# A spectral layer and gated FFN on one core: from unit 8 on, frequency units go in pairs, with a fourth buffer for loaded units

## The chip, the cores and the metric

The kernel runs on one core of a Trainium2 chip. The metric is the device time of one execution in microseconds (us); the core has a matrix engine (PE, with its weight loads shown apart as PEld), a vector engine (DVE), an activation engine (ACT), GpSimd (POOL), and SyncE (SP), which here issues all DMAs. The time before is the median of three runs.

## The reference

```
X = np.fft.rfft(x, axis=1)                      # x: 8 x 3136 x 256
Yr = Xr @ w_r - Xi @ w_i + b_r
Yi = Xr @ w_i + Xi @ w_r + b_i
Yr, Yi = soft-threshold of both at lam = 0.01
y = np.fft.irfft(Yr + 1j * Yi, n=3136, axis=1)
h = np.maximum(y @ w_in, 0.0)                   # 256 -> 1024
conv_out = 3-tap depthwise convolution of h along the sequence
out = (h * sigmoid(conv_out)) @ w_out           # 1024 -> 256
```

The weights of the second half (`w_in`, `conv_w`, `w_out`) arrive as 64-bit floats, which the kernel takes apart as bit patterns on VectorE into a high and a low part.

## The kernel before

The transform of length 3136 is done as 49 by 64. **Stage 1** transforms along 49: for each of 64 *pieces* (8 of them to a batch row) the PE runs `quads` (L333) on a loaded tile `xr`, ACT and DVE copy the two result banks to `a1` (L350, L351), and every second piece is stored to DRAM with three DMAs (L338, L342). **Stage 2** works on *units* of four frequencies: there are 50 (six to a batch row, and one more for each four rows that holds the last frequency). A unit loads its `a2` tile (L371), transforms along 64 on the PE in two halves (L384), and splits the result: ACT copies and casts (`d` L387, `fh` L388), DVE subtracts (`d` L389, `fl` L390), then `third` adds a third plane, on ACT (L395) and POOL (L396). The **mix** multiplies a unit by the complex weights as three planes of 12 matmuls (L412) into three PSUM banks, and DVE joins them to `v` with two additions of the bias (L415) and two of the planes (L417). `shrink` is the soft threshold: two passes of ACT (L428, L429) and one of POOL (L430); the last unit uses `clip` on DVE (L422, L423). **Stage 3** transforms back along 64 (L440, L443) into the pool `psa`, which has one buffer of two banks; ACT copies it to `z1` (L450, two buffers), and DMAs store it (L455, L458). All other PSUM of this part is a ring of six banks, handed out in program order.

`later()` is a generator of *weight steps*: eight pieces of `w_in` and `w_out` of ten DVE steps each, and three short ones for `conv_w`. In the ninth step of a piece DVE subtracts (L279) what ACT has cast in the same step (L278).

The order is written out by hand: engines execute in program order. One turn of the main loop holds stage 3 of unit `it-4`, one or two pieces of stage 1, stage 2 of unit `it`, `shrink` of unit `it-2` and the mix of unit `it-1`. So the mix multiplies what stage 2 made one turn earlier, and three weight steps of DVE stand around the copies of stage 1. Pieces run in turns 1 to 40. From unit 45 on, `last_stage` (stage 4, the way back along 49 for batch row 0, L159; ACT L168, DVE L170) fills the places that pieces had. Then the **FFN** starts: `up` (L656) makes 128 rows of h for two column halves in PSUM (`ps_h`), ACT and DVE make the gate, and `down` (L691) sums into `acc`. Its pools take over the eight PSUM banks: the first `ps_h` lies in banks that were the ring's.

SP issues DMAs in the order of the program too, and waits in front of each for its buffer or its data: whatever is asked later stands behind it.

## Time and profile before

| | us |
|---|---|
| median of 3 runs (1671.15 to 1673.64) | 1672.62 |
| the profiled execution | 1672.12 |
| its span, first to last instruction | 1670.3 |
| PE busy | 1655.1 |
| DVE busy | 1388.5 |
| ACT busy | 1176.6 |
| POOL busy | 192.3 |
| FFN's first matmul (L656) | 468.76 after the span's start |

The profile is of one execution. An engine's busy time is the union of its instructions' records. A row of the timeline gives the start and the length in us of instructions that follow each other, merged when they are alike; the length of a matmul's record reaches past the start of the next, so the pace is read from starts. A row of windows gives, for a stretch, each engine's busy time, the granted clock of the PE (1.00 is full) and the DMA engines' busy share. In the program's names of the profile, digits are left out: `ps_s` is the PSUM tile of stages 1 to 4, `z` of stage 3's store, `a` of stage 1's and of stage 2's load.

### The profile page before, as it was taken

How to read it: one execution, taken by the hardware profiler on the slowest of the kernel's cores; microseconds unless marked ns; L12 is line 12 of the kernel's file. 1: busy time of each engine (PE TensorE's matmuls, PEld its weight loads, DVE VectorE, ACT ScalarE, POOL GpSimd, SP SyncE). 2: the span in 40 equal slices, each digit the busy share in tenths (PEclk: the TensorE clock that was granted, in tenths of full speed). 3: DMA queues.
4: the chain of work that ended last, by engine and by line, in shares of the span. 5: the costliest groups of instructions: out<-in, count | busy, mean ns of one | idle time of the engine just before them, and what ended most of it. 6: DMA issues, size and time to landing. Idle time of an engine off the chain costs nothing.

```text
span 1670.3 us, 30664 instructions
## 1 busy us (share of the span) xinstructions
PE 1655.1 (99%) x12618; PEld 1539.5 (92%) x12618; DVE 1388.5 (83%) x1728; ACT 1176.6 (70%) x1585; POOL 192.3 (12%) x114
## 2 busy tenths in 40 slices
PE   9899999999999999999999999999999999999998
PEld 6688888889999999999999999999999999999998
DVE  3578988877688888888888888888888888888887
ACT  3577777777677777677777776777777776777776
POOL 1444444445300000000000000000000000000000
PEclk9999999999999999999999999999999999999999
DMA  8999999887421101111111011111001111100001
GB/s 219 285 293 283 261 262 275 257 224 195 118 71 52 52 33 42 52 52 42 49 34 44 32 31 52 42 52 52 33 33 52 46 38 52 42 23 23 23 23 45
DMA packets 108297, 162.29 MB, mean 97 GB/s; under 512 B 10842, under 2 KB 87806, under 8 KB 108094
## 3 DMA queue, kind: packets, MB, share of 16 engines
q1 hardware_dynamic: 108158, 160.34, 32.6%
q8 instruction: 100, 1.64, 0.4%
q14 instruction: 39, 0.32, 0.1%
HBM read 83.24 MB, written 77.07 MB: 96 GB/s over the span
## 4 chain that ended last, share of the span: by engine, by line
PE 98%; DMA 1%; issue 0%; ACT 0%; SPq 0%; ACTq 0%
PE acc L691 33%; PE ps_h L656 33%; PE ps_mx L412 13%; PE ps_s L159 7%; PE ps_s L384 6%; PE ps_s L333 3%; PE ps_s L440 3%; PE ps_idle L509 0%; DMA hx<-in_x_dram 0%; DMA a<-sch 0%; PE ps_s L443 0%; DMA sch<-ha 0%; SPq L316 0%; ACT o L697 0%; SPq L319 0%
## 5 line engine op out<-in xcount | busy, mean ns | idle before, releaser
L691 PE MATMUL acc<-wout,gh 128*128 128x256 f32 x3136 | 565.4, 281 | 0.4 <-ACT gh L677 0.4
L672 DVE SCALAR_TENSOR_TENSOR c<-h,cw,c 128x896 f32<-128x896 f32 x448 | 512.8, 1147 | 63.0 <-ACT c L670 61.8
L656 PE MATMUL ps_h<-yh,win 128*128 128x450 f32 (+1 forms) x1792 | 545.0, 365 | 0.0
L691 PEld LDWEIGHTS acc<-wout,gh 128*128 128x128 f32 x3136 | 490.1, 188 | 5.9 <-ACT gh L677 0.6
L691 PE MATMUL acc<-wout,gl 128*128 128x256 f32 x1568 | 434.7, 279 | 0.0
L666 ACT ACTIVATE h<-ps_h 128x898 f32<-128x898 f32 (+1 forms) x224 | 207.2, 925 | 226.7 <-PE ps_h L656 226.4
L656 PEld LDWEIGHTS ps_h<-yh,win 128*128 128x128 f32 x1792 | 337.1, 188 | 24.0 <-issue 0.4
L656 PE MATMUL ps_h<-yl,win 128*128 128x450 f32 (+1 forms) x896 | 327.8, 366 | 0.0
L691 PEld LDWEIGHTS acc<-wout,gl 128*128 128x128 f32 x1568 | 293.3, 188 | 0.2
L674 DVE TENSOR_TENSOR c<-h,c 128x896 f32<-128x896 f32 x224 | 243.4, 1087 | 47.7 <-ACT c L673 46.7
L678 DVE TENSOR_TENSOR gl<-c,gh 128x896 fp32r<-128x896 f32 x224 | 243.2, 1088 | 33.5 <-ACT gh L677 30.1
L677 ACT CAST gh<-c 128x896 fp32r<-128x896 f32 x224 | 210.4, 944 | 81.3 <-DVE c L674 81.1
L673 ACT ACTIVATE c<-c 128x896 f32<-128x896 f32 x224 | 213.5, 954 | 24.1 <-DVE c L672 21.3
L656 PEld LDWEIGHTS ps_h<-yl,win 128*128 128x128 f32 x896 | 168.4, 188 | 10.2
L670 ACT ACTIVATE c<-h,cw 128x896 f32<-128x896 f32 x168 | 175.4, 1044 | 2.9 <-DVE gl L678 0.2
L412 PE MATMUL ps_mx<-wmix_hi,fh 128*128 128x256 f32 x600 | 172.1, 287 | 0.0
L412 PE MATMUL ps_mx<-wmix_lo,fh 128*128 128x256 f32 x600 | 167.6, 279 | 0.0
L412 PE MATMUL ps_mx<-wmix_hi,fl 128*128 128x256 f32 x600 | 167.2, 279 | 0.0
L430 POOL TENSOR_TENSOR r<-r,v 128x1024 f32<-128x1024 f32 x48 | 114.6, 2387 | 217.7 <-ACT v L429 200.1
L384 PEld LDWEIGHTS ps_s<-t,a 128*128 128x128 f32 (+1 forms) x800 | 94.4, 194 | 37.7 <-issue 22.8
L159 PEld LDWEIGHTS ps_s<-i,z 98*128 98x128 f32 x1024 | 122.5, 192 | 2.0 <-issue 0.8
L159 PE MATMUL ps_s<-i,z 98*128 98x98 f32 x1024 | 123.3, 273 | 0.0
(93 smaller groups left out, 1675.7 us busy)
## 6 DMA issues: line engine op xcount, KB each, us to landing
z<-sc SPq DMA_DIRECT2D x64, 392.0 KB
sc<-z SPq DMA_DIRECT2D x96, 256.0 KB
out_dram<-o SPq DMA_DIRECT2D x27, 896.0 KB
xr<-in_x_dram SPq DMA_DIRECT2D x112, 192.0 KB
sc<-a SPq DMA_DIRECT2D x56, 384.0 KB
a<-sc SPq DMA_DIRECT2D x42, 512.0 KB
hx<-in_x_dram SPq DMA_DIRECT2D x16, 192.0 KB
a<-sch SPq DMA_DIRECT2D x6, 512.0 KB
```

The lines of the kernel that those rows point to most:

```text
L159: nc.tensor.matmul(to, z2[:, j, t * P:(t + 1) * P], i2[:, 0 if jg or j else 1, :], start=(j == 0), stop=(j == JG - 1), skip_group_check=True)
L384: nc.tensor.matmul(ps[:, k], a2[0:kk, k, t * P:(t + 1) * P], t2[0:kk, q, :], start=(k == 0), stop=(k == UG - 1), skip_group_check=True)
L412: nc.tensor.matmul(ps[c][:, k, :], lt, rh, start=(n == 0), stop=(n == len(mm) - 1))
L656: nc.tensor.matmul(dst, lt, rh, start=(i == 0), stop=(i == len(mm) - 1))
L666: nc.scalar.activation(hv, src, AF.Relu)
L670: nc.scalar.mul(cv, tap(0), cw[:, 0, f:f + 1])
L672: nc.vector.scalar_tensor_tensor(cv, tap(k), cw[:, k, f:f + 1], cv, op0=ALU.mult, op1=ALU.add)
L673: nc.scalar.activation(c, c, AF.Sigmoid)
L674: nc.vector.tensor_tensor(cv, tap(1), cv, op=ALU.mult)
L677: nc.scalar.copy(gh, c)
L678: nc.vector.tensor_tensor(gl, c, gh.bitcast(F32), op=ALU.subtract)
L691: nc.tensor.matmul(acc[m // 2][:, m % 2, :], lt[:, sl], rh[:, f, :], start=(f == 0 and n == 0 and m % 2 == 0), stop=(f == NF - 1 and n == ...
```

## The change

The loop is cut in three: turns 0 to 7 as before; from unit 8 on one turn takes two units `u` and `u+1`; a drain of its own at the end. In a turn of two, the PE runs stage 3 of `u-4`, up to two pieces, stage 3 of `u-3`, the rest of the pieces, stage 2 of both units, and the mix of **the same** two units. Each unit's `shrink` follows the mix one unit later. The planes of a paired mix are made in the order 0, 1, 2 rather than 2, 0, 1, and the bias is added to planes 0 and 1. Six weight steps a turn stand as three ahead of stage 3's copy, two ahead of the first mix's additions and one between the two mixes. Where there are no pieces, the second stage 3 of a turn takes two banks of the ring in place of `psa`, and so does stage 3 of the last unit. `a2` has four buffers. Loads of `a2` for the next turn are asked ahead of x, and x is asked for once ahead of the pieces and once behind them.

The rows that follow are the order of instructions, engine by engine, as built. **PE**, around unit 12 (`ps_s_1667` is stage 3 of unit 8, `ps_s_1676` to `1683` pieces of stage 1, `ps_s_1706` and `1715` the halves of unit 12's stage 2); before:

```order
L412 MATMUL ps_mx_1623<-wmix_hi,fl 128x256
L440 MATMUL ps_s_1667<-r,i_465 64x256 x8
L333 MATMUL ps_s_1676<-xr,f_118 64x512 x2
L333 MATMUL ps_s_1677<-xr,f_118 64x512 x2
L333 MATMUL ps_s_1682<-xr,f_118 64x512 x2
L333 MATMUL ps_s_1683<-xr,f_118 64x512 x2
L384 MATMUL ps_s_1706<-t_122,a_1559 128x128 x4
L384 MATMUL ps_s_1715<-t_122,a_1559 128x128 x4
L412 MATMUL ps_mx_1730<-wmix_hi,fh 128x256
```

The same place with the change (`ps_s_1717`, stage 3 of unit 8, stands just ahead; `ps_s_1753` is stage 3 of unit 9, `ps_s_1792` to `1824` stage 2 of units 12 and 13, `ps_mx_1841` the first plane of unit 12's mix):

```order
L333 MATMUL ps_s_1726<-xr,f_118 64x512 x2
L333 MATMUL ps_s_1727<-xr,f_118 64x512 x2
L333 MATMUL ps_s_1732<-xr,f_118 64x512 x2
L333 MATMUL ps_s_1733<-xr,f_118 64x512 x2
L457 MATMUL ps_s_1753<-r,i_465 64x256 x8
L333 MATMUL ps_s_1762<-xr,f_118 64x512 x2
L333 MATMUL ps_s_1763<-xr,f_118 64x512 x2
L384 MATMUL ps_s_1792<-t_122,a_1552 128x128 x4
L384 MATMUL ps_s_1801<-t_122,a_1552 128x128 x4
L384 MATMUL ps_s_1815<-t_122,a_1554 128x128 x4
L384 MATMUL ps_s_1824<-t_122,a_1554 128x128 x4
L413 MATMUL ps_mx_1841<-wmix_hi,fh 128x256
```

The matmuls of 64 rows now stand together, and a mix follows the stage 2 that feeds it.

**ACT and DVE**, where the third weight piece comes to its ninth step. ACT before, around unit 17 (`z_2231` is stage 3's copy, L278 the cast of the weights, `ps_s_2245` and `2254` the halves of stage 2):

```order
L450 COPY z_2231<-ps_s_2216 128x1024
L350 COPY a_2236<-ps_s_2225 128x2x256
L278 CAST win_82<-win_m 128x512
L387 COPY d<-ps_s_2245 128x256
L388 CAST fh<-ps_s_2245 128x512
L387 COPY d<-ps_s_2254 128x256
L388 CAST fh<-ps_s_2254 128x512
L428 ACTIVATE r<-v,small 128x1024
```

ACT with the change, at the end of the turn of units 16 and 17 (the first L441 and L442 are `shrink` of unit 15, the second of unit 16, `z_2397` and `z_2424` stage 3's copies of the next turn):

```order
L388 CAST fh<-ps_s_2250 128x512
L395 CAST fh<-d 128x2x256
L441 ACTIVATE r<-v,small 128x1024
L442 ACTIVATE v<-v,small 128x1024
L278 CAST win_82<-win_m 128x512
L441 ACTIVATE r<-v,small 128x1024
L442 ACTIVATE v<-v,small 128x1024
L471 COPY z_2397<-ps_s_2365 128x1024
L350 COPY a_2189<-ps_s_2374 128x2x256
L350 COPY a_2406<-ps_s_2380 128x2x256
L471 COPY z_2424<-ps_s_2409 128x1024
```

DVE at that place with the change (`ps_s_2250` is stage 2 of unit 17, `ps_mx_2268` to `2270` the planes of unit 16):

```order
L390 TENSOR_TENSOR fl<-ps_s_2250,fh 128x512
L271 SCALAR_TENSOR_TENSOR win_rest<-win_r,win_e 128x512
L279 TENSOR_TENSOR win_m<-win_m,win_82 128x512
L417 TENSOR_TENSOR v<-ps_mx_2268,bias 128x512
L417 TENSOR_TENSOR v<-ps_mx_2269,bias 128x512
L420 TENSOR_TENSOR v<-ps_mx_2270,v 128x512 x2
```

The cast L278 moved from behind stage 3's copy to behind a `shrink`, and L279, which needs it, now stands ahead of the additions of a mix.

**ACT where the FFN starts**, with the change (`ps_s_5834` is the last half of stage 4, `ps_s_5843` stage 3 of unit 48 in `psa`, `ps_s_5852` and `5853` the two ring banks of stage 3 of unit 49; in brackets the semaphores waited for):

```order
L168 CAST yh<-ps_s_5834 128x49x4 [waits PE_49]
L168 CAST yh<-ps_s_5834 128x49x4
L471 COPY z_5862<-ps_s_5843 128x1024 [waits DMAHW4_49,DMAHW5_49,PE_49,Activation_49]
L469 COPY z_5866<-ps_s_5852 64x512 [waits DMAHW0_49,DMAHW1_49,PE_49,Activation_49]
L469 COPY z_5866<-ps_s_5853 64x512 [waits PE_49]
```

DMAHW0 and DMAHW1 are the two stores of unit 47's `z`, whose buffer `z_5866` takes. Stage 3 of unit 49 lay in `psa` before, and the FFN's first `ps_h` waited for stage 4's `yh` and `yl` alone; now unit 49 lies in ring banks that `ps_h` takes over, and the first `ps_h` matmul (L727) waits for the last of these copies.

The diff:

```diff
--- before.py
+++ after.py
@@ -178,7 +178,7 @@
         s1p = eb.enter_context(tc.tile_pool(name="s1p", bufs=2, side="right"))
         c0 = eb.enter_context(tc.tile_pool(name="c0", bufs=1, side="right"))
         c1 = ab.enter_context(tc.tile_pool(name="c1", bufs=1))
-        a2p = ab.enter_context(tc.tile_pool(name="a2p", bufs=3))
+        a2p = ab.enter_context(tc.tile_pool(name="a2p", bufs=4))
         cmx = ab.enter_context(tc.tile_pool(name="cmx", bufs=1))
         DB, XRB = 2, 3
         psx = ab.enter_context(tc.tile_pool(name="psx", bufs=6, space=PSUM))
@@ -396,12 +396,13 @@
             nc.gpsimd.tensor_tensor(fl[:, :, 2], d, fh[:, :, 2].bitcast(F32), op=ALU.subtract)
             return fh, fl
 
-        def mix(xs):
+        def mix(xs, paired=False):
 
 
             fh, fl = xs
-            ps = {c: psx.tile([K2, UG // 2, D], F32, name=f"ps_mx{c}", tag="bank") for c in (2, 0, 1)}
-            for c in (2, 0, 1):
+            order = (0, 1, 2) if paired else (2, 0, 1)
+            ps = {c: psx.tile([K2, UG // 2, D], F32, name=f"ps_mx{c}", tag="bank") for c in order}
+            for c in order:
...
             v = wk.tile([K2, 2, UG // 2, D], F32, name="v")
-            for c in range(2):
-                nc.vector.tensor_tensor(v[:, c], ps[2], bias[:, c:c + 1, :].to_broadcast([K2, UG // 2, D]), op=ALU.add)
-            for c in range(2):
-                nc.vector.tensor_tensor(v[:, c], ps[c], v[:, c], op=ALU.add)
+
+            def biased(c, src):
+                nc.vector.tensor_tensor(v[:, c], ps[src], bias[:, c:c + 1, :].to_broadcast([K2, UG // 2, D]), op=ALU.add)
+
+            def joined(c, src):
+                nc.vector.tensor_tensor(v[:, c], ps[src], v[:, c], op=ALU.add)
+            if paired:
+                for c in range(2):
+                    biased(c, c)
+                for c in range(2):
+                    joined(c, 2)
+            else:
+                for c in range(2):
+                    biased(c, 2)
+                for c in range(2):
+                    joined(c, c)
             return v
 
         def clip(v):
@@ -430,24 +443,32 @@
             nc.gpsimd.tensor_tensor(r, r, v, op=ALU.subtract)
             return r
 
-        def stage3_pe(g, r):
-            ps = psa.tile([P, 2, UG // 2, D], F32, name="ps_s3")
+        def stage3_pe(g, r, ring=False):
+            if ring:
+                ps = [psx.tile([P, UG // 2, D], F32, name="ps_s3", tag="bank") for _ in range(2)]
+            else:
+                both = psa.tile([P, 2, UG // 2, D], F32, name="ps_s3")
+                ps = [both[:, h] for h in range(2)]
             for a in range(2):
                 for k in range(UG // 2):
                     for h in range(2):
                         rows = slice(SP * h, SP * (h + 1))
                         if g < NG:
-                            nc.tensor.matmul(ps[SP * a:SP * (a + 1), h, k, :], i1[rows, a, g * UG // 2 + k, :], r[rows, a, k, :],
+                            nc.tensor.matmul(ps[h][SP * a:SP * (a + 1), k, :], i1[rows, a, g * UG // 2 + k, :], r[rows, a, k, :],
                                              start=(k == 0), stop=(k == UG // 2 - 1), skip_group_check=True)
                         else:
-                            nc.tensor.matmul(ps[0:SP, h, k, :], i1[rows, a, U // 2, :], r[rows, a, k, :],
+                            nc.tensor.matmul(ps[h][0:SP, k, :], i1[rows, a, U // 2, :], r[rows, a, k, :],
                                              start=(a + k == 0), stop=(a + k == UG // 2), skip_group_check=True)
-            return ps
+            return ps if ring else both
 
         def stage3_out(b, g, ps):
             z1 = io.tile([P, 2, UG // 2, D], F32, name="z1", bufs=2)
             n = P if g < NG else SP
-            nc.scalar.copy(z1[0:n], ps[0:n])
+            if isinstance(ps, list):
+                for h in range(2):
+                    nc.scalar.copy(z1[0:n, h], ps[h][0:n])
+            else:
+                nc.scalar.copy(z1[0:n], ps[0:n])
             if g < NG:
                 z1 = z1.rearrange("p h k e -> p (h k) e")
                 for c in range(2):
@@ -469,7 +490,7 @@
 
         items = [(b, g) for h in range(B // BH) for b, g in [(h * BH + b, g) for b in range(BH) for g in range(NG)] + [(h * BH, NG)]]
         n_it, n_pc = len(items), B * NX
-        LAG, WP0, LATE, NW, NF0, NF1 = 4, 8, 10, 7, 14, 3
+        LAG, PAIR, WP0, LATE, NW, NF0, NF1 = 4, 8, 8, 10, 7, 14, 3
         xs, vs, ss, a2s, xq, pair = {}, {}, {}, {}, {}, []
         p1 = nx = NX
 
@@ -551,7 +572,7 @@
         wkf.tile([P, 56], F32, name="pad", bufs=1)
         wk.tile([P, 72], F32, name="pad", bufs=1)
         background = later()
-        Y0, Y1 = n_it - 6, n_it - 1
+        Y0 = n_it - 6
         jgs = iter(range(NPC))
 
         def one_by_one():
@@ -568,65 +589,115 @@
             stage4(jg, z2, y0, one_by_one)
             ask_z2()
 
-        for it in range(n_it + LAG):
-            drain = it >= n_it
+        def steps(n):
+            for _ in range(n):
+                next(background, None)
+
+        def s3(i, ring=False):
+            b, g = items[i]
+            return b, g, stage3_pe(g, ss.pop(i), ring)
+
+        def pieces(n):
+            nonlocal p1
+            todo = [next_s1(p1 + i) for i in range(n)]
+            yield
+            for ps in todo:
+                stage1_out(p1, ps)
+                p1 += 1
+
+        for it in range(PAIR):
...
             if it >= LAG:
-                g3 = items[it - LAG]
-                ps3 = stage3_pe(g3[1], ss.pop(it - LAG))
-            n_s1 = min(2 if 0 < it < 5 else (1, 2, 1, 1, 2, 1)[(it - 5) % 6] if it else 0, n_pc - p1)
-            ps1 = [next_s1(p1 + i) for i in range(n_s1)] if it > 1 else []
+                z = s3(it - LAG)
+            n_s1 = 2 if 0 < it < 5 else (1, 2, 1, 1, 2, 1)[(it - 5) % 6] if it else 0
+            if it > 1:
+                out1 = pieces(n_s1)
+                next(out1)
             if it >= LAG:
-                stage3_out(*g3, ps3)
-            if WP0 <= it < Y0:
-                next(background, None)
-            elif it == WP0 - 2:
-                next(background)
-            for ps in ps1:
-                stage1_out(p1, ps)
-                p1 += 1
+                stage3_out(*z)
+            if it == WP0 - 2:
+                steps(1)
+            if it > 1:
+                next(out1, None)
             ask_a2(it + 1)
-            if WP0 <= it < Y0:
-                for _ in range(2):
-                    next(background, None)
-            if it < n_it:
-                xs[it] = stage2(items[it][1], a2s.pop(it))
-            if it == Y0:
+            xs[it] = stage2(items[it][1], a2s.pop(it))
+            if it >= 2:
+                ss[it - 2] = shrink(vs.pop(it - 2))
+            xs[it] = third(xs[it])
+            if it == 1:
+                out1 = pieces(n_s1)
+                next(out1)
+                next(out1, None)
+            if 0 <= it - 3 < NG:
+                fill_inv1(it - 3)
+            if it:
+                vs[it - 1] = mix(xs.pop(it - 1))
+
+        for u in range(PAIR, n_it, 2):
+            busy = u < Y0
+            ask_a2(u + 2, u + 3)
+            fetch(2)
+            if u == LATE:
+                load_t2(NG)
+                load_inv1(NG)
+            n_s1 = min(sum((1, 2, 1, 1, 2, 1)[(i - 5) % 6] for i in (u, u + 1)), n_pc - p1)
+            if u - 3 < NG:
+                fill_inv1(u - 3)
+            z = s3(u - LAG)
+            out1 = pieces(min(n_s1, 2))
+            next(out1)
+            if busy:
+                steps(3)
+            stage3_out(*z)
+            next(out1, None)
+            z = s3(u + 1 - LAG, not n_s1)
+            out1 = pieces(max(n_s1 - 2, 0))
+            next(out1)
+            stage3_out(*z)
+            next(out1, None)
+            ask_a2(u + 2, u + 3)
+            fetch(2)
+            if u == PAIR:
+                ss[u - 2] = shrink(vs.pop(u - 2))
+                vs[u - 1] = mix(xs.pop(u - 1))
+            for i in (u, u + 1):
+                xs[i] = third(stage2(items[i][1], a2s.pop(i)))
+                if u > Y0:
+                    last_stage()
+            if u == Y0:
                 eb.close()
                 zio, y_a = pool("zio", 3, side="right"), pool("y_a", side="right")
                 y0 = new_y(y_a)
                 z2s = []
                 for _ in range(3):
                     ask_z2()
-            if it == n_it - 1:
-                xs[it] = third(xs[it])
-            if 0 <= it - 2 < n_it:
-                ss[it - 2] = (clip if drain else shrink)(vs.pop(it - 2))
-            if it < n_it - 1:
-                xs[it] = third(xs[it])
-            if Y0 < it < Y1:
-                last_stage()
-            if it == 1:
-                for _ in range(n_s1):
-                    stage1_out(p1, next_s1(p1))
-                    p1 += 1
-            if 0 <= it - 3 < NG:
-                fill_inv1(it - 3)
-            if 0 <= it - 1 < n_it:
-                vs[it - 1] = mix(xs.pop(it - 1))
+            ss[u - 1] = shrink(vs.pop(u - 1))
+            if busy:
+                steps(2)
+            vs[u] = mix(xs.pop(u), True)
+            ss[u] = shrink(vs.pop(u))
+            if busy:
+                steps(1)
+            vs[u + 1] = mix(xs.pop(u + 1), True)
+
+        for n in range(2):
+            z = s3(n_it - LAG + n)
+            last_stage()
+            stage3_out(*z)
+            if n == 0:
+                ss[n_it - 1] = clip(vs.pop(n_it - 1))
+            last_stage()
+        z = [s3(n_it - 2 + n, n) for n in range(2)]
+        for q in z:
+            stage3_out(*q)
         assert p1 == n_pc and not z2s and next(background, True)
 
     wk, hp, io, y_b = pool("cwk"), pool("chp", 3), pool("cio"), pool("y_b")
```

More of the change, by code (lines that the diff above doesn't have):

```diff
@@ L576, in spectral_ffn_kernel @@
                 load_t2(it + 2)
-            elif it == LATE:
-                load_t2(NG)
-                load_inv1(NG)
             if 0 <= it - 2 < NG and it % 2 == 0:
@@ L584, in spectral_ffn_kernel @@
                 fill_t2(it + 1)
-            if drain:
-                last_stage()
             if it >= LAG:
-                g3 = items[it - LAG]
-                ps3 = stage3_pe(g3[1], ss.pop(it - LAG))
-            n_s1 = min(2 if 0 < it < 5 else (1, 2, 1, 1, 2, 1)[(it - 5) % 6] if it else 0, n_pc - p1)
-            ps1 = [next_s1(p1 + i) for i in range(n_s1)] if it > 1 else []
-            if it >= LAG:
-                stage3_out(*g3, ps3)
-            if WP0 <= it < Y0:
-                next(background, None)
-            elif it == WP0 - 2:
-                next(background)
@@ L613, in spectral_ffn_kernel @@
                     ask_z2()
-            if it == n_it - 1:
-                xs[it] = third(xs[it])
-            if 0 <= it - 2 < n_it:
-                ss[it - 2] = (clip if drain else shrink)(vs.pop(it - 2))
-            if it < n_it - 1:
-                xs[it] = third(xs[it])
-            if Y0 < it < Y1:
-                last_stage()
-            if it == 1:
-                for _ in range(n_s1):
-                    stage1_out(p1, next_s1(p1))
-                    p1 += 1
-            if 0 <= it - 3 < NG:
-                fill_inv1(it - 3)
-            if 0 <= it - 1 < n_it:
-                vs[it - 1] = mix(xs.pop(it - 1))
+            ss[u - 1] = shrink(vs.pop(u - 1))
[16 more added lines that the diff above has]
+            stage3_out(*q)
         assert p1 == n_pc and not z2s and next(background, True)
```

## The prediction

> **What bounds the kernel now.** I read the page first: the busy shares by slice, the granted clock, the chain of work that ended last.
>
> ```profile
> PE   9899999999999999999999999999999999999998
> PEclk9999999999999999999999999999999999999999
> PE 98%; DMA 1%; issue 0%; ACT 0%; SPq 0%; ACTq 0%
> L333 PE MATMUL ps_s<-xr,f 49*64 49x512 f32 x448 | 58.4, 594 | 6.9 <-issue 6.3 <-PE ps_s L384 0.5
> 304.08:329.19 25.11, 25.11 (x238) 21.16 (x237) 21.09 (x37) 18.78 (x29) 11.45 (x7) 1.00 0.88 254
> ```
>
> The PE is busy from end to end and its clock nearly always full, and 98% of the chain is PE. The row of groups says that stage 1 (L333) never waited for an `xr` in flight; the waits view shows nothing for the PE from unit 8 to the FFN. The last row is three units of the middle in the view of windows: PE 25.11 of 25.11 us, DVE 21.09, ACT 18.78, DMA engines 0.88 busy. So no wait can be removed. The change can gain only where matmuls that follow each other cost more than their own pace, and it can lose wherever DVE, ACT or a DMA, each with some 15 to 25% to spare, now comes later than the PE wants it.
>
> **What the change removes: changeovers of the PE.** The timeline, starts and lengths:
>
> ```profile
> 303.75 0.28 PE L412 MATMUL ps_mx<-wmix_lo,fh 128*128 128x256 f32 x1
> 303.87 0.28 PE L412 MATMUL ps_mx<-wmix_hi,fl 128*128 128x256 f32 x1
> 304.08 1.11 PE L440 MATMUL ps_s<-r,i 64*64 64x256 f32 x16
> 305.00 1.05 PE L333 MATMUL ps_s<-xr,f 49*64 49x512 f32 x8
> 305.98 2.05 PE L384 MATMUL ps_s<-t,a 128*128 128x128 f32 x16
> 307.79 0.36 PE L412 MATMUL ps_mx<-wmix_hi,fh 128*128 128x256 f32 x1
> 307.99 0.28 PE L412 MATMUL ps_mx<-wmix_lo,fh 128*128 128x256 f32 x1
> ...
> 386.73 1.11 PE L440 MATMUL ps_s<-r,i 64*64 64x256 f32 x16
> 387.77 2.05 PE L384 MATMUL ps_s<-t,a 128*128 128x128 f32 x16
> ...
> 305.98 0.38 PE L384 MATMUL ps_s<-t,a 128*128 128x128 f32 x1
> ...
> L384 PE MATMUL ps_s<-t,a 128*128 128x128 f32 x768 | 99.6, 284 | 0.9 <-DMA a<-sch 0.9
> ```
>
> A unit has one change from tiles of 128 rows (the mix) to tiles of 64 (stage 3, stage 1), and one back (to stage 2). From the start of a mix's last matmul to stage 3 are 304.08 − 303.87 = 0.21 us, where matmuls of the mix follow each other after 303.87 − 303.75 = 0.12: 0.09 lost. Sixteen matmuls of stage 3 take 387.77 − 386.73 = 1.04 ahead of stage 2 and 305.00 − 304.08 = 0.92 ahead of stage 1: 0.12 lost. The first matmul of stage 2 lasts 0.38 against a mean of 0.284: 0.10 more. Sure is 0.09 + 0.12 = 0.21, all three are 0.31, and some 0.05 may lie in the slower first matmuls of stage 3, which this view doesn't part: 0.36 at most. I take 0.34, near the three. A turn of two units saves one such pair: stage 2 to stage 2, mix to mix, and stage 3 among the pieces stay in one size of tile. That is 21 turns, and one more in the drain, where stage 3 of units 48 and 49 stand together: 22 × 0.34 = **7.5 us** (22 × 0.21 = 4.6 to 22 × 0.36 = 7.9). Nothing else of the PE's work is changed in number.
>
> **What it adds: waits.** The mix now multiplies what stage 2 has just made. Stage 2 as it went before, from its start S = 305.98:
>
> ```profile
> 307.23 0.37 ACT L387 COPY d<-ps_s 128x256 f32<-128x256 f32 x1 [0.45 <-PE ps_s L384]
> ...
> 308.34 0.59 ACT L388 CAST fh<-ps_s 128x512 fp32r<-128x512 f32 x1
> ...
> 308.18 0.42 DVE L389 TENSOR_TENSOR d<-ps_s,d 128x256 f32<-128x256 f32 x1 [0.37 <-issue]
> ...
> 309.45 0.68 DVE L390 TENSOR_TENSOR fl<-ps_s,fh 128x512 fp32r<-128x512 f32 x1
> ```
>
> ACT's splits run from S + 1.25 to S + 2.95, and DVE's, one behind the other, from S + 2.2 to 309.45 + 0.68 = S + 4.15. Unit u's mix starts two stages 2 later, at S + 2 × (307.79 − 305.98) = S + 3.62. Its first matmul takes 0.20 and the next ones 0.12 each, so the sixth, the first to take the second half's `fl`, is due at S + 4.3, and its weight load, which carries `fl`, 0.12 earlier. So `fl` and the need for it meet within 0.05 us. DVE's steps ahead of it (stage 1's copies, three weight steps) are over by then on an even turn, or up to 0.2 late. I take 0.08 a turn: 21 × 0.08 = **1.7** (0 to 21 × 0.25 = 5). Behind ACT's splits of u come those of u+1, behind DVE's too; their mix is due 2.9 us later and is covered.
>
> Stage 3 of the turn's second unit uses the one buffer of `psa`, and so waits for ACT's copy of the first one's. That copy stands behind two `shrink`s.
>
> ```profile
> 305.28 1.01 ACT L450 COPY z<-ps_s 128x1024 f32<-128x1024 f32 x1 [1.73 <-PE ps_s L440]
> ...
> 308.81 1.16 ACT L428 ACTIVATE r<-v,small 128x1024 f32<-128x1024 f32 x1
> 310.01 1.15 ACT L429 ACTIVATE v<-v,small 128x1024 f32<-128x1024 f32 x1
> ...
> L417 DVE TENSOR_TENSOR v<-ps_mx,v 128x512 f32<-128x512 f32 x100 | 67.7, 684 | 14.8 <-PE ps_mx L412 14.8
> ...
> L278 ACT CAST win<-win_m 128x512 fp32r<-128x512 f32 x4 | 2.5, 630 | 0.0
> L279 DVE TENSOR_TENSOR win_m<-win_m,win 128x512 f32<-128x512 f32 x4 | 2.7, 685 | 2.5 <-ACT win L278 2.5
> ```
>
> From the first mix's start M: a mix is 312.17 − 307.79 = 4.4 us; its last plane is whole at about M + 4.5, DVE's two joins (2 × 0.68, L417) end at M + 5.9, the two passes of `shrink` (1.16 + 1.15) at M + 8.3. Stage 3 of u−4 starts after both mixes, at M + 8.5 or so, ends at M + 9.5, and its copy (1.01) at M + 10.7. With two pieces between (each 305.98 − 305.00 = 0.95) stage 3 of u−3 is due at M + 8.5 + 0.9 + 1.8 = M + 11.2, after it. Where the ninth step of a weight piece is one of the two ahead of the mix's additions, the order shown above has L278 behind a whole `shrink` on ACT and L279 ahead of L417 on DVE: the additions start some 3 us late, `shrink` ends some 2 us late, and the copy at M + 12.4, so that stage 3 waits 1.2 or so. This is so for the third and the sixth of the eight pieces (one with fewer pieces of stage 1 behind it, half of that). In the turn with one piece left it is due at M + 10.3 and waits 0.5. Sum **2.4** (0.5 if DVE gets ahead in time, 4 if each lasts twice as long).
>
> The start of the FFN:
>
> ```profile
> 463.90 1.11 PE L440 MATMUL ps_s<-r,i 64*64 64x256 f32 x16
> 464.93 2.03 PE L159 MATMUL ps_s<-i,z 98*128 98x98 f32 x16
> 466.89 1.94 PE L443 MATMUL ps_s<-r,i 64*64 64x256 f32 x16
> 468.76 0.47 PE L656 MATMUL ps_h<-yh,win 128*128 128x448 f32 x1
> ...
> 446.76 1.08 SPq L455 DMA_DIRECT2D sc<-z  x2
> ...
> 449.50:450.50 1.00, 1.00 (x11) 1.00 (x10) 1.00 (x3) 1.00 (x2) 0.59 (x1) 1.00 0.41 156
> 450.50:451.50 1.00, 1.00 (x10) 1.00 (x10) 1.00 (x2) 0.97 (x2) 0.71 (x1) 1.00 0.00 0
> ```
>
> Let T be the start of unit 47's stage 3. Then come two stages 4 (466.89 − 464.93 = 1.96 each), stage 3 of 48 and 49 (0.92 + 1.87), and the PE is free for `ps_h` at T + 1.04 + 3.9 + 2.8 = T + 7.7. On ACT unit 47's copy stands behind four casts of the stage 4 before and the first of the next, and ends at about T + 4.6. Its buffer's next user, the copy of unit 49, waits for both stores. A pair of stores (446.76) left the DMA engines idle some 3.7 us after it was asked: 0.41 busy in the slice from 449.50, 0.00 in the next. So unit 49's two half copies start at T + 8.4 and end 2 × 0.59 later (a copy of 512 elements from PSUM is as long as L388 above), at T + 9.6; `ps_h` waits for them, as it lies in their banks. **2.0 us** of a wait that was not there (1 to 3: what the stores take).
>
> The fourth `a2` buffer and the earlier requests take nothing off the PE, which did not wait for `a`; moved weight steps are the same DVE work. What they could cost is rival C.
>
> Sum: −7.5 + 1.7 + 2.4 + 2.0 = −1.4. Against the profiled execution, 1672.12, that is 1670.7; the median lies 0.50 above it, so **1671.2 us**.
>
> **Rivals.** *A, no waits but the last.* DVE is idle 16% of a unit and makes `fl` in time; the weight steps fall well; the gain stands against the FFN's 2.0 and some 1: 1672.6 − 7.5 + 3.0 = 1668.1. For it: `fl` is due within 0.05 us of its making, and the bounds at zero. Against: two of the waits follow from program order alone. Chance 0.26.
>
> *B, the clock.* The PE's idle time at the FFN's start could cost more than itself:
>
> ```profile
> 7.40:10.80 3.40, 1.93 (x12) 0.42 (x8) 0.93 (x2) 0.58 (x1) 0.00 (x0) 1.00 1.01 200
> 10.90:17.60 6.70, 6.70 (x70) 5.11 (x70) 1.38 (x2) 1.17 (x2) 0.00 (x0) 0.50 1.00 243
> ...
> 41.60:45.00 3.40, 2.38 (x16) 0.93 (x15) 0.00 (x0) 0.75 (x2) 1.14 (x2) 1.00 1.03 324
> ```
>
> Here 3.40 us with the PE 1.93 busy were followed by 6.7 at a granted clock of 0.50; 3.40 us with 2.38 busy still ran at full clock. [...] Half the clock for 6.8 us is up to 3.4 us more: 1674.6. Chance 0.22. [...]
>
> *C, x comes late, slower.*
>
> ```profile
> 303.85 2.77 SPq L316 DMA_DIRECT2D xr<-in_x_dram  x4
> 306.67 0.56 SPq L319 DMA_DIRECT2D xr<-in_x_dram  x1
> ```
>
> Such a load holds two pieces, in one of three buffers. Eight pieces pass in six units, 2 × 25.11 us, so two pieces in 12.6. When a load is asked, at least one buffer is still full: 12.6 less 3.4 to ask it and some 3.7 to land (as the stores above) leaves a lead of at least 5.5 us. The change asks `a2` of the next two units ahead of x, and where a batch row begins, those wait for the last stores of stage 1, with x behind them on SP: if each of the two waits a whole landing, 2 × 3.7 = 7.4 us, x is up to 1.9 late; I price it at half, 1 us, at the five row starts that follow unit 8: 1671.2 + 5 = 1676.2. It decides from a delay of 5.5 us. For it: the DMA share of 0.88. Against: stage 1 never waited for x under way, and x is asked twice a turn. Chance 0.10. That the change doesn't do what it says is excluded by the rows of the order.
>
> **How the numbers follow.** Forecast 0.42, A 0.26, B 0.22, C 0.10. About 0.2%, 3.3 us, is what a measurement can tell from no change. Faster by more than that means below 1669.3: all of A and a little of the forecast's range (0.01), 0.27. Slower means above 1675.9: C (0.10) and the half of B where other terms come out high (0.10), 0.20. The rest is 0.53. The forecast's own range, by the bounds of its terms, is 1668 to 1674.5; A's lower end (gain 7.9, costs 2) is 1667, C's middle with a little more 1677. So 1667 to 1677.
>
> **What would show it.** Two mixes side by side in the timeline, and stage 3 to stage 2 with one changeover a turn. Waits of the PE's weight loads for DVE's `fl`, some 0.1 each; of stage 3 for ACT's `z`, one or two near 1 us; of the first `ps_h` for ACT's `z`, about 2. A wait of L279 for L278 in the first half, twice 2 us. The FFN's first matmul at about 467.4 in place of 468.76. Granted clock 0.50 right behind it would be B; any wait of L333 for DMA `xr` would be C. Wrong would be the prediction most of all if the changeovers gave less than 0.2 a pair, or if waits of `fl` ran to 0.5 a turn.

## The result, and the profile after

| | before | with the change |
|---|---|---|
| median, us | 1671.88 | 1694.51 (1692.65 to 1698.16) |
| ratio, 95% interval | | 1.0138 (1.0124 to 1.0152) |
| span of the profiled execution, us | 1670.3 | 1691.0 |
| the FFN's first matmul, us from the start | 468.76 | 487.91 |
| the span behind it, us | 1201.5 | 1203.1 |

The change makes the kernel 22.6 us slower; 1671.2 was predicted, with 1677 as the upper end. Of the span's 20.7 us, 19.15 lie ahead of the FFN and 1.6 right behind its start. The page of the changed kernel:

```profile
PE   8899999999999999999999999999999999999998
PEclk9899999999999999999999999999999999999999
PE 89%; DVE 4%; DMA 2%; issue 2%; ACT 1%; SPq 1%; POOL 0%; ACTq 0%; DVEq 0%
PE 1660.4 (98%) x12618; PEld 1547.2 (91%) x12618; DVE 1407.1 (83%) x1726; ACT 1180.7 (70%) x1592; POOL 193.0 (11%) x115
```

The slices of the PE look nearly as before; it is the chain that tells. It was 98% PE, and is 89%, with DVE, DMA, SP and ACT in the rest: the PE now waits. DVE is busy 18.6 us longer than before (1388.5), with two instructions fewer: the kernel before clips its last two units on DVE, not only the last, and unit 48's clip (1.9 us) is now a `shrink` on ACT and POOL.

The view of waits of the PE (total us, times, the longest):

```profile
PE ps_s L457 <- ACT z L471: 4.1, 8, 1.1
PE ps_h L727 <- ACT z L469: 3.6, 1, 3.6
PE ps_s L333 <- DVE a L351: 2.5, 2, 2.0
PE ps_s L333 <- DVE win L280: 1.3, 1, 1.3
PE ps_s L333 <- DMA xr<-in_x_dram: 1.3, 1, 1.3
...
```

The names behind L333 are not to be taken at their word: one says DMA, the others name DVE instructions that have nothing to do with stage 1. A weight step (L280) releases no `xr` and no PSUM bank. Where the named releaser makes no sense, the starts must be read, stretch by stretch. I took the starts of the PE's phases from the timeline, turn by turn, and set each phase against the undisturbed turn of the same trace, that of unit 12:

```profile
139.63 1.11 PE L457 MATMUL ps_s<-r,i 64*64 64x256 f32 x16
140.54 1.91 PE L333 MATMUL ps_s<-xr,f 49*64 49x512 f32 x16
142.26 1.09 PE L457 MATMUL ps_s<-r,i 64*64 64x256 f32 x16
143.13 1.09 PE L333 MATMUL ps_s<-xr,f 49*64 49x512 f32 x8
144.15 3.84 PE L384 MATMUL ps_s<-t,a 128*128 128x128 f32 x32
```

From start to start this is stage 3 0.91, two pieces 1.72, stage 3 0.87, one piece 1.02, two stages 2 3.59, two mixes 8.58 us (the next turn starts at 156.32), together 16.7. A turn of three pieces took 17.02 before (304.08 to 321.10), one of two pieces 16.21 where it is 15.83 when nothing waits: the changeovers do give 0.32 to 0.38 a turn, as predicted. What eats it:

| excess over the undisturbed turn | places | us |
|---|---|---|
| between stage 3 and the second group of pieces | turns of units 14, 20, 26, 32, 38 | 1.55 + 2.23 + 1.51 + 1.02 + 0.77 = 7.1 |
| in these second groups | the same | 0.9 |
| in the first group of pieces | turns of 18 and 28 | 3.33 + 2.45 = 5.8 |
| stage 3 for `psa` | turns of 10, 14, 20, 24, 30, 34, and of 40 | 2.96 + 0.46 = 3.4 |
| a mix for `fl` | six turns, 0.08 to 0.41 | 1.7 |
| stage 2 for a bank | turns of 24 and 30 | 0.9 |
| the FFN's first matmul | once | 3.6 |
| the clock, behind the longest waits | three places | 1.6 + 1.6 + 1.6 = 4.8 |

Together 28.2. The measured loss is 20.7, which leaves 7.5 for the changeovers; 22 of them at 0.32 to 0.38 are 7.0 to 8.4. The clock's share is told apart by the pace of the matmuls behind a wait. (Stage 3 of unit 24, in the turn of unit 28, takes 0.9 longer than others in both kernels; that is not counted.)

**x is late.** At the turn of unit 14, PE and SP:

```profile
159.47 1.11 PE L457 MATMUL ps_s<-r,i 64*64 64x256 f32 x16 [0.32 <-ACT z L471]
161.89 1.35 PE L333 MATMUL ps_s<-xr,f 49*64 49x512 f32 x8 [1.31 <-DVE win L280]
...
154.46 2.60 SPq L316 DMA_DIRECT2D xr<-in_x_dram  x4
157.10 0.55 SPq L319 DMA_DIRECT2D xr<-in_x_dram  x1
```

Stage 3 starts at 159.47 and should be done with at 160.34; stage 1 starts at 161.89. The last DMA of the x that it needs was asked at 157.10 and landed, by the trace's DMA records, at 161.80. In the turn of unit 20 the last x landed at 217.97, and stage 1 starts at 218.11.

**Two turns, behind units 16 and 26, stumble over a weight step.** DVE, ACT, POOL and PE there:

```profile
189.21 2.48 DVE L279 TENSOR_TENSOR win_m<-win_m,win 128x512 f32<-128x512 f32 x1 [2.30 <-ACT win L278]
191.62 1.27 DVE L417 TENSOR_TENSOR v<-ps_mx,bias 128x512 f32<-128x512 f32 x2
192.81 1.27 DVE L420 TENSOR_TENSOR v<-ps_mx,v 128x512 f32<-128x512 f32 x2
195.81 1.27 DVE L420 TENSOR_TENSOR v<-ps_mx,v 128x512 f32<-128x512 f32 x2
197.00 2.23 DVE L264 TENSOR_SCALAR win_e<-win_bits 128x512 int32<-128x512 int32 x1
...
188.57 0.60 ACT L278 CAST win<-win_m 128x512 fp32r<-128x512 f32 x1
...
188.75 2.40 POOL L443 TENSOR_TENSOR r<-r,v 128x1024 f32<-128x1024 f32 x1 [0.68 <-ACT v L442]
196.59 2.36 POOL L443 TENSOR_TENSOR r<-r,v 128x1024 f32<-128x1024 f32 x1 [5.44 <-ACT v L442]
...
192.50 1.52 PE L333 MATMUL ps_s<-xr,f 49*64 49x512 f32 x8
194.19 2.23 PE L333 MATMUL ps_s<-xr,f 49*64 49x512 f32 x8 [0.17 <-PE ps_s L333]
197.55 0.68 PE L457 MATMUL ps_s<-r,i 64*64 64x256 f32 x8 [1.14 <-ACT z L471]
```

DVE waits 2.30 us for ACT's cast, as foreseen. Then L279 itself lasts 2.48 where it lasted 0.685 before, and ends 0.5 behind POOL's pass (188.75 + 2.40 = 191.15); L264 at 197.00 does the same beside the next pass. The mixes' additions end at 197.1, the mixes' PSUM banks come free one by one, and stage 1, which takes its banks from the same ring, runs at DVE's pace: its second piece starts at 194.19, 0.1 after the additions L420 of 192.81 end. Of the 3.33 us lost here, 1.14 are stage 3's wait for `psa` (the last row); the other 2.2 are stage 1's. Behind unit 26 it is 1.13 of 2.45.

**The FFN's start**, PE, ACT and SP:

```profile
482.43 1.89 PE L460 MATMUL ps_s<-r,i 64*64 64x256 f32 x16
487.91 0.47 PE L727 MATMUL ps_h<-yh,win 128*128 128x448 f32 x1 [3.59 <-ACT z L469]
...
486.80 1.06 ACT L469 COPY z<-ps_s 64x512 f32<-64x512 f32 x2 [3.04 <-DMA sc<-z]
...
481.34 1.09 SPq L476 DMA_DIRECT2D sc<-z  x2
```

Unit 47's stores are asked at 481.34, the T + 4.6 of the prediction (T is 476.73), but the copy that waits for them starts 5.4 us later, not 3.7.

**The clock**, by windows (PE busy, and the granted clock, third number from the end):

```profile
219.24:224.40 5.16, 5.16 (x33) 5.16 (x32) 2.57 (x5) 2.70 (x6) 0.00 (x0) 0.67 1.08 319
...
487.90:494.70 6.80, 6.79 (x26) 6.12 (x27) 2.10 (x5) 0.95 (x2) 0.00 (x0) 0.75 0.21 59
```

Behind idle times of 1.99 and 3.59 us the PE ran at less than full clock for some microseconds (0.50 from 219.74 to 223.15 and from 489.39 to 492.80; once more from 291.42 to 294.83, behind a wait of 1.13 ahead of stage 3 in the turn of unit 28): stage 2 of the turn of unit 20 took 5.22 in place of 3.59, and the first 60 matmuls of the FFN 13.88 in place of 12.30.

### The profile page after: what moved, and what is told of

Read it like the earlier page. It is cut to its first block, busy times and chain, and to the rows that moved or that the text cites. A ratio compares the mean times of both kernels' runs of the same rounds, so it can differ in the third digit from the quotient of the medians.

```text
span 1691.0 us, 30716 instructions
## 1 busy us (share of the span) xinstructions
PE 1660.4 (98%) x12618; PEld 1547.2 (91%) x12618; DVE 1407.1 (83%) x1726; ACT 1180.7 (70%) x1592; POOL 193.0 (11%) x115
## 3 DMA queue, kind: packets, MB, share of 16 engines
q1 hardware_dynamic: 108158, 160.34, 32.7%
## 4 chain that ended last, share of the span: by engine, by line
PE 89%; DVE 4%; DMA 2%; issue 2%; ACT 1%; SPq 1%; POOL 0%; ACTq 0%; DVEq 0%
PE acc L762 32%; PE ps_h L727 32%; PE ps_mx L413 9%; PE ps_s L159 7%; PE ps_s L384 5%; PE ps_s L333 2%; PE ps_s L457 2%; DMA xr<-in_x_dram 1%; DVE v L420 1%; DVE fl L390 0%; SPq L316 0%; DVE a L351 0%; DMA hx<-in_x_dram 0%; ACT r L441 0%; DVE v L417 0%
## 5 line engine op out<-in xcount | busy, mean ns | idle before, releaser
L727 PE MATMUL ps_h<-yh,win 128*128 128x450 f32 (+1 forms) x1792 | 546.2, 366 | 3.6 <-ACT z L469 3.6
L727 PEld LDWEIGHTS ps_h<-yh,win 128*128 128x128 f32 x1792 | 338.0, 189 | 27.8 <-ACT z L469 4.0
L727 PE MATMUL ps_h<-yl,win 128*128 128x450 f32 (+1 forms) x896 | 328.5, 367 | 0.0
L727 PEld LDWEIGHTS ps_h<-yl,win 128*128 128x128 f32 x896 | 168.8, 188 | 10.3
```

Of the source, the lines that this page charges most:

```text
L727: nc.tensor.matmul(dst, lt, rh, start=(i == 0), stop=(i == len(mm) - 1))
```

## The experiments

The first theory was that three separate waits (x, the cast, the last unit's bank) and the clock behind them are the loss, and its rival that DVE, held up by POOL, is behind all of them. Each kernel is the changed one with the edit shown, unless the text says on what it builds. The ratio is to the kernel before, measured beside it on the same chip. Where a text says how much earlier the FFN starts, it compares two traces, and these differ already at the start of the turn of unit 8, ahead of all paired turns: 101.88 in the changed kernel, 101.96 before, 100.20 to 102.30 in the others.

**x asked behind the first pieces too**

```
             next(out1, None)
+            fetch(1)
             z = s3(u + 1 - LAG, not n_s1)
```

> The changed kernel, and x is asked a third time in each turn, behind the first group of pieces. Theory: the five waits of the PE ahead of the second group of pieces (1.5, 2.2, 1.5, 1.0 and 0.8 us, every third turn) are for x whose buffer is free since the first group but which SP asks only behind the whole turn's stores. They go, and the half clock behind the longest with them (1.6): 1694.5 becomes about 1686, and the PE's gap between stage 3 and stage 1 is under 0.3 us everywhere. Rival: the gap is for a PSUM bank that DVE's late copies of stage 1 give back; then x is earlier, the gaps stay, and the time is 1693 to 1696.

Measured: 1687.41 us, ratio 1.0097 (1.0075 to 1.0118), and the FFN starts at 478.91, 9.0 earlier (7.7 counted from the turn of unit 8, with a wait at the FFN's start of 4.0). All five gaps are gone, as in the turn of unit 14:

```profile
158.14 1.11 PE L457 MATMUL ps_s<-r,i 64*64 64x256 f32 x16 [0.32 <-ACT z L471]
159.03 1.09 PE L333 MATMUL ps_s<-xr,f 49*64 49x512 f32 x8
```

Stage 1 follows stage 3's start after 0.89. A gap of 0.9 is new in the long turn of unit 18. The rival falls: DVE's copies stand where they stood.

**x ahead of a2**

```
-            ask_a2(u + 2, u + 3)
             fetch(2)
+            ask_a2(u + 2, u + 3)
```

(at both places)

> The changed kernel with both requests of x ahead of those of a2. By the mechanism of the prediction's rival C (x stands behind a2 loads that wait for stores) this alone takes the five waits for x away, some 7 us: 1686 to 1688. By the theory that x is asked too late because the buffer's release is looked for only once a turn, behind the pieces, a2 is not ahead of it where it counts, and the time stays within 1 us of 1694.5.

Measured: 1689.57, ratio 1.0107 (1.0087 to 1.0128), between the two forecasts. The gaps fall to 0.9, 0, 1.0, 0.3 and 0.3 us, and one of 0.9 is new. So both hold: a2 ahead of x costs some, and that the free buffer is looked for only behind the turn's pieces costs the rest. How much is which is rough, as these gaps differ between traces of kernels that ask for x alike: 4.8 (units 48 and 49 exchanged) to 9.0 us (the cast ahead) in sum.

**The cast ahead of the shrink**

```
-            ss[u - 1] = shrink(vs.pop(u - 1))
             if busy:
                 steps(2)
+            ss[u - 1] = shrink(vs.pop(u - 1))
```

> The changed kernel, with the two weight steps ahead of a mix's additions (and so ACT's cast L278) issued ahead of the shrink rather than behind it. Theory: in the turns of units 16 and 26 DVE's L279 no longer waits 2.3 us for that cast, and the turns behind them (191.59 and 285.24, 3.3 us too long in stage 1 each, and 1.6 at half clock behind the second) are as long as others: 1694.5 becomes about 1686. Rival: stage 1 there is late because POOL's pass keeps DVE's weight steps waiting (2.2 to 2.5 us in place of 0.7), which this edit does not touch: 1692 or more.

Measured: 1686.11, ratio 1.0081 (1.0062 to 1.01). The turns of units 18 and 28 take 17.5 and 16.7 us in place of 20.3 and 20.9. But x is now later elsewhere (the turn of unit 20 takes 23.7, was 21.2). DVE at the place:

```profile
185.46 1.70 DVE L279 TENSOR_TENSOR win_m<-win_m,win 128x512 f32<-128x512 f32 x1
187.08 1.28 DVE L417 TENSOR_TENSOR v<-ps_mx,bias 128x512 f32<-128x512 f32 x2
```

No wait ahead of L279, and yet 1.70 long: here it stands beside POOL's L396 (185.05, 1.56 long). The FFN starts 7.7 earlier in this trace, but not for the cast alone: 1.7 are there at the turn of unit 8, and the first `ps_h` starts at 480.18 without a wait. It is the second that waits for unit 49's copy, by 1.43.

**Units 48 and 49 exchanged**

```
-        z = [s3(n_it - 2 + n, n) for n in range(2)]
+        z = [s3(n_it - 2 + n, not n) for n in range(2)]
```

> The changed kernel, with stage 3 of unit 48 in the ring's banks and that of unit 49 in psa, the other way round. Theory: the first matmul of the FFN waits for the last copy out of ring banks; unit 48's copy waits for unit 46's stores, done long before, so the wait of 3.6 us at the FFN's start is below 0.7, and the half clock behind it (1.6 us) goes: 1694.5 becomes about 1689.5. Rival: unit 49, now behind unit 47's copy out of psa, waits as long on the PE, or ps_h needs psa's banks as early: no gain.

Measured: 1685.87, ratio 1.0085 (1.0065 to 1.0104).

```profile
478.47 1.89 PE L460 MATMUL ps_s<-r,i 64*64 64x256 f32 x16
480.30 0.47 PE L727 MATMUL ps_h<-yh,win 128*128 128x448 f32 x1
```

The FFN starts with no wait, and its first 60 matmuls take 12.99 us in place of 13.88. The gain of some 8.6 us is more than the 5 expected. The rest of it lies ahead, where the edit does not reach: the turn of unit 8 starts 1.5 earlier in this trace, and x is late by 4.8 in sum in place of 7.1. The waits for x vary from run to run by some microseconds; so single runs of these kernels differ by more than those of the kernel before.

**POOL's pass cut short**

This kernel leaves most of the subtraction out, and its output is not the layer's.

```
-            nc.gpsimd.tensor_tensor(r, r, v, op=ALU.subtract)
+            nc.gpsimd.tensor_tensor(r[:, 0, 0, 0:8], r[:, 0, 0, 0:8], v[:, 0, 0, 0:8], op=ALU.subtract)
```

> The changed kernel, but POOL's third part of shrink (L443, 2.39 us) subtracts 8 of 1024 elements; the rest of r is left without the negative half. Theory: a weight step of DVE that meets this pass lasts until the pass ends (2.1 to 2.5 us in place of 0.4 to 0.7; DVE busy 1407.1 against 1388.5 before). Then no weight step lasts over 1.7 us, DVE's busy time falls by 12 to 20 us, and the PE's waits that go through DVE shrink: 1694.5 becomes 1686 to 1691. Rival: the steps are long for a reason of their own, and the time stays above 1692.

Measured: 1685.21 (1677.23 to 1686.46), ratio 1.0055 (1.003 to 1.0081). By groups and by engine:

```profile
PE 1654.7 (98%) x12618; PEld 1544.9 (92%) x12618; DVE 1371.4 (81%) x1726; ACT 1181.1 (70%) x1592; POOL 86.3 (5%) x115
...
L279 DVE TENSOR_TENSOR win_m<-win_m,win 128x512 f32<-128x512 f32 x4 | 2.8, 688 | 2.3 <-ACT win L278 2.3
```

and in the changed kernel itself:

```profile
L279 DVE TENSOR_TENSOR win_m<-win_m,win 128x512 f32<-128x512 f32 x4 | 6.0, 1498 | 2.3 <-ACT win L278 2.3
```

DVE's busy time falls by 35.7 us (1407.1 to 1371.4), though not one of its instructions was taken away. That is more than the 12 to 20 expected, and 17.1 less than in the kernel before, whose weight steps must have met the pass as well. L279 is back at 0.688; its wait for the cast, 2.3, is untouched. Every pair of mixes from unit 10 on now takes 8.58: the waits for `fl` were POOL's doing. The first pieces in the turns of units 18 and 28 lose 1.5 and 0.7 us in place of 3.3 and 2.5. The half microseconds for `psa`, the waits for x and that of the FFN (3.5) are still there. So both theories hold, each for its own waits.

**The three edits together**

> The changed kernel with the three edits together that were tried alone: x asked also behind the first pieces, the cast ahead of the shrink, units 48 and 49 exchanged between psa and the ring. If the three waits are separate, their gains add up: the FFN's first matmul moves from 487.9 by 9.0, 7.7 and 3.6 us to about 468, and the time is 1670 to 1674. If they share a cause (DVE late, say), the sum falls short: 1677 or more.

Measured: 1673.79, ratio 1.0009 (0.9999 to 1.002), the FFN at 469.43. The three kinds of wait are gone together: the second stage 3 lasts 0.86 to 0.89 wherever pieces follow it, the first pieces behind units 16 and 26 lose 0.3 and nothing, and the first `ps_h` does not wait. The time is inside the range for separate waits, though that range was reached by counting the FFN's 3.6 twice, since the 7.7 of the cast's run hold it already. Counted from the turn of unit 8, the FFN starts 18.9 earlier than in the changed kernel; by place, x gives 8.2 (7.7 and the longer wait of that run), the two turns 7.0 and the FFN 3.6, together 18.8. What is left are the waits of half a microsecond.

**The steps behind stage 3's copy as well**

```
-            if busy:
-                steps(3)
             stage3_out(*z)
+            if busy:
+                steps(3)
```

> As the three edits together, and the three weight steps of a turn behind stage 3's copy on ACT, not ahead of it. Theory: the half us by which the second stage 3 waits for psa, in the turns of units 10, 14, 20, 24, 30 and 34, is the cast L278 (0.60) that stands ahead of the copy of z there. Six waits of 0.5 go: 3 us under the three edits, 1667 to 1671, and the first group of stage 1 lasts 1.72 in place of 2.23 in these turns. Rival: the copy is late because shrink is; then 2.23 stays.

Measured: 1673.11, ratio 1.0005 (0.9996 to 1.0015), no difference. The reason held: the first group takes 1.72 in all six turns. But the mixes wait for `fl` instead (9.0 to 9.7 us in six turns in place of 8.58), and stage 2 for banks. The wait was moved, not removed.

**2, 2, 2 in turns of two pieces**

```
-                steps(3)
+                steps(n_s1 if n_s1 > 1 else 3)
...
-            z = s3(u + 1 - LAG, not n_s1)
+            z = s3(u + 1 - LAG, n_s1 < 2)
...
+            if busy:
+                steps(2 if n_s1 == 2 else 1)
             ss[u] = shrink(vs.pop(u))
-            if busy:
-                steps(1)
```

(on top of the edit before; `fetch(1)` stays)

> As four, and in turns of two pieces the six weight steps go 2, 2, 2 (in place of 3, 2, 1), the last ones ahead of the shrink too, and stage 3 takes ring banks where one piece is left. Theory: in turns of two pieces DVE comes late to fl by 0.4 us because three steps stand ahead of two copies; two steps ahead leave it in time. Some 5 waits of 0.4 and one of 0.46 go: 2 us under four, 1665 to 1669, faster than the kernel before. Rival: fl waits for ACT's casts; no difference from four.

Measured: 1673.29, ratio 1.0008 (0.9998 to 1.0018): a miss. The FFN starts 2.4 earlier than in the kernel it builds on, half of it (1.25) there at the turn of unit 8, and the median shows nothing of it. The mixes of turns of two pieces still take up to 9.2.

**The steps behind the first group's copies, alone**

```
-            if busy:
-                steps(3)
             stage3_out(*z)
             next(out1, None)
+            if busy:
+                steps(3)
```

> The changed kernel, and nothing but this: the three weight steps of a turn stand behind the first group's copies of stage 1. Theory: by itself this takes the waits of 0.35 to 0.56 us for psa, for fl and for a bank of stage 2, some 6 us in all; x late at the row starts, the long turns behind units 16 and 26 and the wait at the FFN's start stay: 1686 to 1689. Rival: it only helped with x in time and the cast ahead; 1691 or more.

Measured: 1681.52, ratio 1.0058 (1.0035 to 1.008), more than expected. All pairs of mixes from unit 10 on take 8.58, the first groups of two pieces 1.72 (but for the two long turns), and DVE's busy time is 1390.5. The two long turns are there as before. The other two larger waits are smaller in this trace: x is late at three places (2.2, 2.0 and 1.1), and the first `ps_h` does not wait (it starts at 476.77), only the second:

```profile
480.26 0.47 PE L727 MATMUL ps_h<-yh,win 128*128 128x448 f32 x1 [0.77 <-ACT z L469]
```

In this kernel and in that of the cast, it is the second `ps_h` that waits for unit 49's copy; why the banks fall otherwise there is not shown. So not all of this run's gain is the steps'.

**All of it**

The three edits, the steps behind the first group's copies, and ring banks where one piece is left (`n_s1 < 2`).

> The three edits, and the three weight steps of a turn behind the first group's copies of stage 1 on DVE (so behind stage 3's copy and the group's copies on ACT too), and ring banks for the second stage 3 where one piece is left. Theory: POOL's pass of shrink holds up the weight steps, and the copies of stage 1 stood behind them; now the copies come first, the pass ends meanwhile, and the waits of stage 2 for a bank that L351 gives back (0.35 to 0.8 a turn) and of the second stage 3 (0.5 each in six turns) go: 4 to 6 us under the three edits, 1667 to 1670. Rival: the steps now delay fl, and the mixes grow by as much: 1672 to 1675.

Measured: 1667.82 (1664.25 to 1670.09), ratio 0.9973 (0.9963 to 0.9984): faster than both kernels, 0.27% faster than the one before. The page of the fastest of these runs, and a turn in the timeline:

```profile
PE 98%; DMA 1%; issue 0%; SPq 0%; ACT 0%; DVE 0%; ACTq 0%
PE 1646.7 (99%) x12618; PEld 1541.2 (93%) x12618; DVE 1389.1 (84%) x1726; ACT 1181.2 (71%) x1593; POOL 193.1 (12%) x115
...
154.08 1.11 PE L457 MATMUL ps_s<-r,i 64*64 64x256 f32 x16
154.99 1.91 PE L333 MATMUL ps_s<-xr,f 49*64 49x512 f32 x16
156.71 1.11 PE L457 MATMUL ps_s<-r,i 64*64 64x256 f32 x16
157.60 1.09 PE L333 MATMUL ps_s<-xr,f 49*64 49x512 f32 x8
158.61 3.84 PE L384 MATMUL ps_s<-t,a 128*128 128x128 f32 x32
...
460.30 0.47 PE L728 MATMUL ps_h<-yh,win 128*128 128x448 f32 x1
```

The chain is 98% PE again, every pair of mixes from unit 10 on takes 8.58, and only two of the paired turns lose 0.2 or more (0.26 and 0.20). The FFN starts at 460.30, 8.5 us ahead of the kernel before; 1.4 of that is there at the turn of unit 8 (100.59 against 101.96), and 7.1 is what the changeovers give less the small waits.

**The other three steps moved too**

```
-            if busy:
-                steps(2)
             ss[u - 1] = shrink(vs.pop(u - 1))
             vs[u] = mix(xs.pop(u), True)
+            if busy:
+                steps(3)
             ss[u] = shrink(vs.pop(u))
-            if busy:
-                steps(1)
```

> As six, but the other three steps stand between the two mixes' additions, none ahead of the first. Theory: POOL's first pass overlaps the two steps ahead of the additions and so delays shrink and stage 3's copy; behind the additions they meet its end: equal to six or up to 2 us faster. Rival: the second mix's PSUM banks come free later, and stage 1 of the next turn waits: slower than six by 2 us or more.

Measured: 1691.95, ratio 1.0116 (1.0101 to 1.0132). The waits of the PE:

```profile
PE ps_s L333 <- DVE v L417: 10.8, 13, 1.2
```

Stage 1 waits for the second mix's banks, once in each of 13 turns. Three DVE instructions a turn in another place cost 24 us against the kernel above (1691.95 to 1667.82).

**The changed kernel again**

> The changed kernel once more, beside the others: 1692 to 1697 by the first measurement; by the theory the five waits for x, the two long turns and the wait at the FFN's start are there again, of about the same size.

Measured: 1692.35, ratio 1.0121 (1.0102 to 1.0141). Four gaps for x, 3.3, 1.5, 1.8 and 1.0 us (five the first time), the long turns, and 3.9 at the FFN's start.

## Why the prediction was wrong

- **Changeovers, −7.5: right.** Undisturbed turns are 0.32 to 0.38 us shorter than two units before, and from the turn of unit 8 to the FFN the kernel with all the edits is 7.1 us shorter than the kernel before.
- **The mix behind its own stage 2, +1.7: right in size** (1.7), but by luck: it was put down to a near meeting of `fl` and the need for it in every turn, and six turns waited, 0.08 to 0.41; with POOL's pass cut short none of the mixes from unit 10 on waits.
- **Stage 3 for `psa`, with the blocked weight step, +2.4: this wait was right, and a larger one beside it was missed.** The two turns, the cast behind the shrink, DVE's wait (2.30 against "some 3") and stage 3's (1.14 and 1.13 against 1.2 and half of it) were as foreseen. The step that failed is the end of that chain: "so that stage 3 waits 1.2 or so" was taken for the whole loss. It took L279 at 0.685 when it lasts 2.48 beside POOL, and it followed the delay to `psa` alone, not to the ring: the late additions also keep the mixes' banks, from which stage 1 takes its own, and stage 1 lost 2.2 and 1.3 more. That gave 5.8 us in two turns, not about 2, and 1.6 of clock; with POOL's pass cut short it gave 2.2. Of the half microseconds for `psa` elsewhere, the 0.46 in the turn of unit 40 was foreseen (0.5); the other six, 3.0 in all, are ACT's cast ahead of the copy, which the prediction did not look for in the turns of units 10, 14 and so on.
- **The FFN's start, +2.0: right in kind.** The wait was 3.6, as the two stores took 5.4 us, with the DMA engines 0.97 busy, and not the 3.7 of a quieter stretch (0.54 busy); then came the clock.
- **x, +0 in the forecast: wrong, and the largest miss.** This was rival C, given 0.10 and 5 us at five places; it costs 8.0 at five places, and 1.6 of clock. The lead of "at least 5.5 us" was not there: the last request for the x of the turn of unit 14 stood at 157.10 and landed 4.7 later ("some 3.7"), 1.5 after stage 1 was due. Its mechanism, a2 ahead of x, is half of it or somewhat more; the rest is what "x is asked twice a turn" passed over: between the two requests no buffer is looked for, though one falls free in the middle of a turn.
- **The clock: rival B, right in kind.** Waits of 2.0 and 3.6 us were followed by a lowered clock; with a third place, behind a wait of 1.13, that is 4.8 us. The prediction's sum has 6.8 us at half clock, as long as a stretch at 0.50 in the kernel before (48.40 to 55.20); that much was not shown behind a wait like these: the three stretches at 0.50 lasted 3.41 each and cost 1.6. The length of a wait alone does not decide it here: a wait of 1.66 was followed by the lowered clock (the cast ahead, at 270.73; 0.57 from 272 to 276), one of 1.85 was not (units 48 and 49 exchanged, at 160.98; 1.00 from 161 to 171):

```profile
272.00:276.00 4.00, 4.00 (x22) 4.00 (x23) 1.71 (x3) 2.05 (x5) 0.00 (x0) 0.57 1.09 295
...
161.00:171.00 10.00, 10.00 (x85) 9.19 (x86) 7.26 (x14) 6.90 (x13) 2.60 (x2) 1.00 1.07 306
```

- **The range** was also narrower than the prediction's own working: the upper bounds of its terms, −4.6 + 5 + 4 + 3, add up to 7.4 over the kernel before, or 1680, not 1674.5. The measured time lies beyond that too.
- Common to all: the terms were priced one by one, each at the kernel's old durations. DVE, at 21.09 of 25.11 us, had 4 to spare, and lost up to 1.8 of them at each meeting of a weight step with POOL.

Which DVE instructions POOL held up and which it did not is read from two rows of the changed kernel, DVE and POOL, and two of the kernel before:

```profile
154.21 1.27 DVE L420 TENSOR_TENSOR v<-ps_mx,v 128x512 f32<-128x512 f32 x2
...
153.48 2.41 POOL L443 TENSOR_TENSOR r<-r,v 128x1024 f32<-128x1024 f32 x1 [0.67 <-ACT v L442]
...
126.14 2.39 POOL L430 TENSOR_TENSOR r<-r,v 128x1024 f32<-128x1024 f32 x1 [4.28 <-ACT v L429]
127.78 1.30 DVE L280 TENSOR_TENSOR win<-win_m,win_rest 128x512 fp32r<-128x512 f32 x1
```

The two additions L420, with one input in PSUM, run within POOL's pass in their usual 0.68 each (starts 0.6 apart), and so do all 119 additions of the changed kernel that meet a pass (0.67 to 0.69); L279, with both inputs in SBUF, did not: 2.48 with the pass, 0.688 with it cut short. The kernel before has the same: L280 starts 1.6 into the pass, ends 0.5 behind it, and loses 0.6. With the change some steps start 0.4 to 0.8 into the pass and lose 1.4 to 1.8. L264, which has one input in SBUF, was held up as well (2.23 in place of 0.42). What in the hardware parts the two kinds was not shown. The prediction took no account of POOL's pass.

## What to carry to other kernels

When engines run in program order, a regrouping that helps one engine must be replayed on the others: for each moved instruction look at what it waits for, at everything queued behind it, and at which buffers or banks those give back. Requests for data belong right behind the instruction that frees the buffer, not at the turn's end. Put a slow helper's work beside instructions that it does not disturb (here the additions, 0.68 within POOL's pass as elsewhere), and price the moved ones at the duration that they have beside their new neighbours (here up to 2.48 for L279, not 0.685).

## What was not expected of the hardware

DVE's weight steps of 128x512 on SBUF that started within POOL's pass of `shrink` lasted until 0.3 to 0.6 us behind its end: the four L279 of `win` took 0.685 us before, 1.498 on average with the change, up to 2.48, and 0.688 with that pass cut short; DVE's busy time went 1388.5, 1407.1, 1371.4 with it. A wait of the PE of 1.99 us was followed by a granted clock that averaged 0.67 from 219.24 to 224.40 (0.50 from 219.74 to 223.15), and one of 1.85 with units 48 and 49 exchanged was not (1.00 over the next 10 us).
